# Retention in pairs of units, k tokens left out, and a shorter float64 conversion in a kernel of retention and two feed-forward layers

## The chip, the core and the metric

The kernel runs on one core of a Trainium2 chip, in one launch. The metric is the device time of that launch in microseconds, the median of several runs. The core's engines are named as in the profile: PE (matmul) with PEld (its weight loads), DVE (VectorE), ACT (ScalarE), POOL (GpSimd) and SP (SyncE, here only a queue of DMAs). 16 DMA engines move data.

## What is computed

Batch 4, 8 heads, 768 tokens, head size 64; then two feed-forward layers on 3072 tokens of width 512, inner width 2048, in float32:

```python
gamma = 1.0 - 2.0 ** (-5.0 - np.arange(H))
for t in range(S):
    state = gamma[None, :, None, None] * state + np.einsum('bhd,bhe->bhde', k[:, :, t], v[:, :, t])
    y[:, :, t] = scale * np.einsum('bhd,bhde->bhe', q[:, :, t], state)
x = y.transpose(0, 2, 1, 3).reshape(B * S, H * D)
h = x @ w_in;   x = (h * (1.0 / (1.0 + np.exp(-1.702 * h)))) @ w_out       # first layer
h = x @ w_in2;  x = (np.maximum(h, 0.0) ** 2) @ w_out2                     # second layer
```

q, k and v come as float32, the four weight matrices as float64.

## The kernel before

**Retention.** It runs over 24 units of 128 tokens (`NU`; six, `CPB`, in each of four batch rows). A unit's data are 2048 float32 words in each of 128 partitions, 1 MB: words 0 to 1023 are q and k transposed (`qk`), 1024 to 1535 the k tokens (`kn`), 1536 to 2047 v. `load_unit` (L462) brings them in two DMAs of 512 KB on SP's queue into one of five buffers (`UNITS`), and the load of unit u + 4 stands behind the outputs of unit u - 1. `scores(u)` (L489) makes the products of k and q (`sc`, 16 matmul instructions on 64 rows by 128 columns), the masked copy `pt` on DVE, and `vs`, v times a decay, on POOL for units below 6 and every third one, else on ACT as eight small multiplications. `outputs(u)` (L547) makes on PE: `yp` from `vs` and `pt` (array shape 128 by 64), the growth of the state `dp` from `kn` and `vs` (128 by 64; not for the sixth unit of a batch row, whose state no one reads), which ACT copies to `st`, and the part of `yp` across units from `st` and q (64 by 64; not for the first unit of a batch row). `scaled` multiplies `yp` on DVE by a table into the layer's input: `x0` for block 0 (split by `split_0` into `hl`), `xs` or `xout` for the others. The loop at L610 does scores(u), then outputs(u - 1). In PSUM `sc` has one buffer and `yp` two.

**Weights.** A float64 word is turned into float32 from its two 32-bit halves. `scale_words` (L131) scales the upper half as a float and the lower half as an integer, both on ACT; `join` (L138) shifts and masks the upper half and then puts the sign back, two DVE operations; `round_up` (L150) adds the lower half, a third. `cv_high` (ACT) and `cv_low` (DVE) split the result into two fp32r parts, hi and lo, in `w`. The first layer has 32 such slices (`order`), loaded by POOL's queue (`cv_load`, 512 KB each, five buffers `raw`). `cv_unit` (L193) does the steps of one slice over three units from unit 7 on (`CV0`), six slices in all during the retention; the other 26 are done by `cv_step` (L216) beside block 0.

**First layer.** Blocks 0 and 1 of 512 tokens go through `up` (L647: 12 matmuls, gelu and its copy on ACT, the rest `gl` on DVE) and `down` (L676: 12 matmuls, two steps behind), 16 steps each. In block 0 each step calls `cv_step` twice, every fourth step once. Slices of `up(f)` are number 2f - 1 of `order`, those of `down(f)` number 2f + 2. After that, blocks of 1024 tokens run in a product scheme with seven products for eight quadrants (`up2`, `down2`); their operands are made by `make_first` and `make_second` beside the earlier blocks, in pieces that `background` draws by credit in us. `make_second` (L331) converts the 32 slices of the second layer's weights with the same `scale_words`, `join` and `round_up`. Its 384 and 128 columns have opposite signs.

The order on each engine is the order in which the code is written (`tc.manual_schedule`); the waits between engines follow from tiles and their buffers.

Of the kernel before, what the change touches and what calls it, by code (L numbers as in the profile page):

```python
# [19 lines left out]
P = 128  # L20
# [13 lines left out]
UNITS = 5  # L34
# [11 lines left out]
CV0 = 7  # L46
RAWU = 2
# [17 lines left out]
def tile_retention_then_two_ffns(  # L65
# [65 lines left out]
    def scale_words(hm, raw, n=512):  # L131

        nc.scalar.mul(hm[:, 0:n], raw[:, 0:n, 1].bitcast(F32), 2.0 ** -112)
        if n < 512:
            nc.scalar.mul(hm[:, n:512], raw[:, n:512, 1].bitcast(F32), -2.0 ** -112)
        nc.scalar.mul(raw[:, :, 0], raw[:, :, 0], 2.0 ** -29)  # L136

    def join(out, hb):  # L138

        v.tensor_scalar(  # L140
            out=out, in0=hb, scalar1=3, scalar2=0x7FFFFFFF,
            op0=ALU.logical_shift_left, op1=ALU.bitwise_and,
        )
        yield
        v.scalar_tensor_tensor(
            out=out, in0=hb, scalar=0x80000000, in1=out, op0=ALU.bitwise_and, op1=ALU.bitwise_or
        )
        yield

    def round_up(w, raw):  # L150

        half = w.bitcast(U16).rearrange("p (c t) -> p c t", t=2)[:, :, 0]
        v.scalar_tensor_tensor(out=half, in0=half, scalar=65527.0, in1=raw[:, :, 0], op0=ALU.min, op1=ALU.add)
# [24 lines left out]
    def convert():  # L178
# [7 lines left out]
        for _ in join(hm.bitcast(U32), raw[:, :, 1]):  # L186
            yield
# [5 lines left out]
    def cv_unit(u):  # L193

        cv["step"] += 1
        part = (u - CV0) % 3
        if part == 2:
            cv_low()
        elif part == 1 and half:
            next(half.pop(), None)  # L200
        elif part == 0 and u >= CV0 and cv["b"] < cv["a"]:
            half.append(convert())
            next(half[0])
            next(half[0])

    def cv_ahead(u):

        if u == 21:
            cv["ahead"] = RAWS
        if u >= RAWU and (u - RAWU) % 3 == 0 or u > 21:  # L210
            cv_load()
        n = cv["a"]
        if n < min(cv["load"], cv["b"] + 2) and cv["step"] >= loaded[n] + 4:
            cv_a()

    def cv_step(f=None):  # L216
# [3 lines left out]
        if cv["b"] < cv["a"]:  # L220
            for _ in convert():
                pass
# [108 lines left out]
    def make_second():  # L331

        with (
# [27 lines left out]
            for n in range(len(jobs)):  # L361
# [5 lines left out]
                hb = hm.bitcast(U32)  # L367
                w = pool.tile([P, 8, P], F32, tag="w", name=f"w32_{n}")
                wf = w.rearrange("p q c -> p (q c)")[:, 0:512]
                wu = wf.bitcast(U32)  # L370
# [841 lines left out]
```

## Time and profile before

| what | us |
|---|---|
| median of 3 runs | 1033.64 (1032.73 to 1034.77) |
| profiled execution, own time | 1033.87 |
| its span, first to last instruction | 1031.8 |
| PE busy | 1021.9 (99%), 5575 matmul records |
| PEld busy | 843.6 (82%) |
| DVE busy | 770.2 (75%) |
| ACT busy | 579.0 (56%) |
| POOL busy | 111.5 (11%) |

PE's busy time is a union of matmuls that overlap in the pipeline, so 99% says that it seldom stood with nothing under way, not that it ran at its peak. The profile names the granted clock of TensorE: 1.0 of full speed (2.4 GHz, the upper of its two levels) in all 40 slices of the span. The span has three parts: the retention to 82.8 us, blocks 0 and 1 of the first layer, and the blocks of the product scheme. In the retention the rows to look at are PE's groups and the DMA share; behind it, what the weight loads (PEld) waited for, since all other idle time of the other engines costs nothing.

### The profile page before, as it was taken

What the parts mean: (1) busy time and instruction counts of PE and PEld (TensorE: products, weight loads), DVE (VectorE), ACT (ScalarE), POOL (GpSimd) and SP (SyncE); (2) the same over time, 40 slices, a digit from 0 to 9 for tenths busy, and PEclk for the clock granted to TensorE, in tenths of its full rate; (3) what the DMA queues carried; (4) which work ended last, traced back from release to release, by engine and by line L of the source; (5) the groups of instructions that cost most, each with busy time, mean ns of one, the idle gap of its engine ahead of it and who ended that gap; (6) DMA issues with size and microseconds to landing.
All of it is one profiled execution on the core that took longest, in us unless ns stands there. A gap on an engine that the chain in (4) does not pass through costs nothing.

```text
span 1031.8 us, 15634 instructions
## 1 busy us (share of the span) xinstructions
PE 1021.9 (99%) x5575; PEld 843.6 (82%) x5575; DVE 770.2 (75%) x1033; ACT 579.0 (56%) x960; POOL 111.5 (11%) x167
## 2 busy tenths in 40 slices
PE   8999999999999999999999999999999999999998
PEld 6888888888888888888888888888888888888886
DVE  5888998798888888666888776886455986455953
ACT  4767775344667565566655798564233464334443
POOL 3121110111322000211001211000000001000000
PEclk9999999999999999999999999999999999999999
DMA  9994797866879887999886999867666867766664
GB/s 356 407 398 173 263 314 296 320 229 242 308 233 373 300 293 233 363 368 364 269 289 228 389 381 307 261 221 237 214 194 191 266 223 235 216 192 194 213 195 163
DMA packets 118669, 281.38 MB, mean 273 GB/s; under 512 B 12608, under 2 KB 12736, under 8 KB 118336
## 3 DMA queue, kind: packets, MB, share of 16 engines
q1 hardware_dynamic: 93200, 186.95, 54.3%
q0 software_dynamic: 24672, 92.28, 24.9%
q10 hardware_dynamic: 720, 1.15, 0.3%
q8 instruction: 44, 0.72, 0.3%
q14 instruction: 33, 0.27, 0.1%
HBM read 206.93 MB, written 73.40 MB: 272 GB/s over the span
## 4 chain that ended last, share of the span: by engine, by line
PE 80%; DVE 2%; ACT 1%; DMA 1%; issue 0%; DVEq 0%
PE D L893 36%; PE X L893 17%; PE Z L893 8%; PE Y L893 4%; PE y L685 2%; PE y L684 2%; PE y L683 2%; PE h L652 2%; PE h L654 1%; PE h L653 1%; PE h L856 1%; PE h L855 1%; PE h L854 1%; DMA r<-kw 1%; DVE wq L350 0%
## 5 line engine op out<-in xcount | busy, mean ns | idle before, releaser
L893 PE MATMUL D<-gx,r 128*128 128x512 f32 x1680 | 383.5, 389 | 0.1
L893 PEld LDWEIGHTS D<-gx,r 128*128 128x128 f32 x1680 | 314.9, 188 | 67.0 <-DVE gx L998 1.2
L998 DVE TENSOR_TENSOR gx<-g,gx 128x1024 fp32r<-128x1024 f32 x140 | 170.9, 1223 | 43.9 <-ACT gx L997 43.4
L997 ACT CAST gx<-g 128x1024 fp32r<-128x1024 f32 x140 | 146.0, 1054 | 95.1 <-PE D L893 91.8
L893 PE MATMUL X<-xh,r 128*128 128x512 f32 x576 | 177.9, 390 | 0.3 <-ACT g L911 0.2
L911 ACT COPY g<-X 128x512 f32<-128x512 f32 x108 | 63.4, 587 | 153.6 <-PE X L893 153.6
L916 DVE TENSOR_TENSOR g<-Z,g 128x512 f32<-128x512 f32 x72 | 49.7, 690 | 128.8 <-ACT g L911 98.7
L893 PEld LDWEIGHTS X<-xh,r 128*128 128x128 f32 x576 | 107.7, 188 | 24.2 <-ACT g L911 1.8
L893 PE MATMUL X<-xl,r 128*128 128x512 f32 x288 | 112.0, 389 | 0.0
L893 PE MATMUL Z<-xh,r 128*128 128x512 f32 x288 | 88.7, 389 | 0.0
L893 PEld LDWEIGHTS X<-xl,r 128*128 128x128 f32 x288 | 54.0, 188 | 11.4
L893 PEld LDWEIGHTS Z<-xh,r 128*128 128x128 f32 x288 | 54.1, 188 | 11.2
L893 PE MATMUL Z<-xl,r 128*128 128x512 f32 x144 | 56.0, 389 | 0.0
L652 PE MATMUL h<-hl,w 128*128 128x512 f32 x128 | 50.1, 392 | 0.3 <-DVE w L173 0.2
L653 PE MATMUL h<-hl,w 128*128 128x512 f32 x128 | 49.9, 390 | 0.0
L654 PE MATMUL h<-hl,w 128*128 128x512 f32 x128 | 49.8, 389 | 0.0
L685 PE MATMUL y<-gl,w 128*128 128x512 f32 x128 | 49.8, 389 | 0.0
L683 PE MATMUL y<-gh,w 128*128 128x512 f32 x128 | 49.8, 389 | 0.0
L684 PE MATMUL y<-gh,w 128*128 128x512 f32 x128 | 49.8, 389 | 0.0
L351 POOL DMA_DIRECT2D kw<-wq x32 | 30.3, 947 | 151.4 <-DVE w L382 75.0
L893 PE MATMUL Y<-xh,r 128*128 128x512 f32 x144 | 44.3, 389 | 0.0
L136 ACT ACTIVATE raw<-raw 128x512 uint32<-128x512 uint32 x64 | 43.0, 672 | 0.0
(112 smaller groups left out, 1548.2 us busy)
## 6 DMA issues: line engine op xcount, KB each, us to landing
r<-kw SPq DMA_DIRECT2D x532, 256.0 KB, 3.3
kw<-wq POOLq DMA_DIRECT2D x32, 896.0 KB, 7.1
unit<-qkv SPq DMA_DIRECT2D x48, 512.0 KB, 9.1
raw<-w POOLq DMA_DIRECT2D x32, 512.0 KB, 6.2
kw<-wh POOLq DMA_DIRECT2D x16, 1024.0 KB, 4.7
kw<-w SPq DMA_DIRECT2D x16, 512.0 KB, 4.7
raw<-win POOLq DMA_DIRECT2D x16, 512.0 KB, 6.8
raw<-wout POOLq DMA_DIRECT2D x16, 512.0 KB, 7.9
```

Source lines behind the costliest of these rows:

```text
L136: nc.scalar.mul(raw[:, :, 0], raw[:, :, 0], 2.0 ** -29)
L652: nc.tensor.matmul(hp, lo[:, k], xh, start=(k == 0), stop=False)
L653: nc.tensor.matmul(hp, hi[:, k], xh, start=False, stop=False)
L654: nc.tensor.matmul(hp, hi[:, k], xl, start=False, stop=(k == KD - 1))
L683: nc.tensor.matmul(a, lo[:, e], gh, start=s0, stop=False)
L684: nc.tensor.matmul(a, hi[:, e], gh, start=False, stop=False)
L685: nc.tensor.matmul(a, hi[:, e], gl, start=False, stop=s1)
L893: nc.tensor.matmul(a, w, b, start=start, stop=stop, skip_group_check=True)
L911: nc.scalar.copy(out=t, in_=a)
L916: v.tensor_tensor(out=t, in0=a, in1=t, op=ALU.add)
L997: nc.scalar.copy(out=hi, in_=src)
L998: v.tensor_tensor(out=lo, in0=src, in1=hi, op=ALU.subtract)
```

## The change

- The retention goes over groups: units 0 and 1 alone, then pairs. Both scores of a pair stand together, then the outputs of the pair before, in the order: state of its first unit, values of both, state of the second, across for both. `sc` has two buffers, one for even and one for odd units; `yp` has one, of twice the use: both units of a pair share the tile. `pt` and `vs` have four buffers. `vs` of even units goes to POOL, of odd ones to ACT (units below 6 all to POOL).
- Eight units may be held instead of five; five of each eight lie in buffers of the weight pool `wa`, free at that time. A unit's load is split at the tile border, and for the sixth unit of a batch row the k tokens are not loaded.
- The conversion uses a parametric relu (one ACT pass that scales positive and negative upper halves differently, so that the shift brings the sign in its place), one shift on DVE, and one operation that scales and adds the lower half's upper 16 bits. ACT passes over the lower half are gone.
- Four slices are converted in the retention, one per group from group 8 on; in block 0 each step calls `cv_step` twice. The credit that `make_second` reports for a slice is 1.65 instead of 1.85 us.

```diff
-UNITS = 5
+UNITS = 8
+WIDE = 5
-CV0 = 7
-RAWU = 2
+CV0 = 8
+RAWU = 4
+CONV = 4
...
     def scale_words(hm, raw, n=512):
-        nc.scalar.mul(hm[:, 0:n], raw[:, 0:n, 1].bitcast(F32), 2.0 ** -112)
-        if n < 512:
-            nc.scalar.mul(hm[:, n:512], raw[:, n:512, 1].bitcast(F32), -2.0 ** -112)
-        nc.scalar.mul(raw[:, :, 0], raw[:, :, 0], 2.0 ** -29)
+        for a, z, scale in ((0, n, 2.0 ** -112), (n, 512, -2.0 ** -112)):
+            if a < z:
+                nc.scalar.activation(
+                    out=hm[:, a:z], in_=raw[:, a:z, 1].bitcast(F32), func=ACTF.Prelu, scale=scale, alpha=-2.0 ** 32
+                )
     def join(out, hb):
-        v.tensor_scalar(
-            out=out, in0=hb, scalar1=3, scalar2=0x7FFFFFFF,
-            op0=ALU.logical_shift_left, op1=ALU.bitwise_and,
-        )
-        yield
-        v.scalar_tensor_tensor(
-            out=out, in0=hb, scalar=0x80000000, in1=out, op0=ALU.bitwise_and, op1=ALU.bitwise_or
-        )
-        yield
+        v.tensor_scalar(out=out, in0=hb, scalar1=3, scalar2=None, op0=ALU.logical_shift_left)
...
-        v.scalar_tensor_tensor(out=half, in0=half, scalar=65527.0, in1=raw[:, :, 0], op0=ALU.min, op1=ALU.add)
+        half = halves(w.bitcast(U16))[:, :, 0]
+        low = raw.bitcast(U16).rearrange("p c (t u) -> p c t u", u=2)[:, :, 0, 1]
+        v.scalar_tensor_tensor(out=half, in0=low, scalar=2.0 ** -13, in1=half, op0=ALU.mult, op1=ALU.add)
...
-    def cv_unit(u):
+    def cv_group(k):
         cv["step"] += 1
...
+        cv_low()
+        if k >= CV0 and cv["b"] < min(cv["a"], CONV):
+            convert()
+    def cv_ahead(k):
+        if k >= RAWU:
             cv_load()
         n = cv["a"]
-        if n < min(cv["load"], cv["b"] + 2) and cv["step"] >= loaded[n] + 4:
+        if n < min(cv["load"], cv["b"] + 2) and cv["step"] >= loaded[n] + 2:
             cv_a()
...
-                    units[u] = att.tile([P, 2048], F32, tag="unit", name=f"unit{u}", bufs=UNITS)
+                    units[u] = [
+                        wa_p.tile([P, 1024], F32, tag=f"w{i}", name=f"unit{u}_{i}")
+                        if u % UNITS >= UNITS - WIDE
+                        else att.tile([P, 1024], F32, tag=f"unit{i}", name=f"unit{u}_{i}", bufs=UNITS - WIDE)
+                        for i in range(2)
+                    ]
...
+                    if a == 1024 and u % CPB == CPB - 1:
+                        a = 1536
...
-                if u == 1:
-                    sc = aps.tile([P, 2, NP, P], F32, tag="yp", name="sc1")
-                else:
-                    sc = aps.tile([P, 2, NP, P], F32, tag="sc", name=f"sc{u}", bufs=1)
+                sc = aps.tile([P, 2, NP, P], F32, tag=f"sc{u % 2}", name=f"sc{u}", bufs=1)
...
-                if u < CPB or u % 3 == 0:
+                if u < CPB or u % 2 == 0:
...
-                yp = aps.tile([P, 2, NP, P], F32, tag="yp", name=f"yp{u}")
+                yp = aps.tile([P, 2, NP, P], F32, tag="yp", name=f"yp{pair[0]}", bufs=1)
...
+                grow(pair[0])
+                for g, u in enumerate(pair):
+                    within(g, u)
+                for u in pair[1:]:
+                    grow(u)
+                for g, u in enumerate(pair):
+                    across(g, u)
...
-            for u in range(NU + 1):
-                cv_high()
-                masked = scores(u) if u < NU else None
+            groups = [(0,), (1,)] + [(u, u + 1) for u in range(2, NU, 2)]
+            for k, group in enumerate(groups + [()]):
+                masks = [scores(u) for u in group]
...
                 low = split_0()
-                scaled = outputs(u - 1) if u > 0 else None
+                before = groups[k - 1] if k > 0 else ()
+                scaled = outputs(before) if before else None
...
+                cv_high()
+                for masked in masks:
                     masked()
                 if low is not None:
                     low()
-                cv_unit(u)
+                cv_group(k)
                 if scaled is not None:
                     scaled()
-                cv_ahead(u)
-                if u > 0:
-                    load_unit(u + UNITS - 1)
+                cv_ahead(k)
+                for u in before:
+                    load_unit(u + UNITS)
...
                 cv_step(low)
-                if f % 4 < 3:
-                    cv_step()
+                cv_step()
...
-                steps = join(wu, hb)
-                next(steps)
-                yield 0.45
-                next(steps)
-                yield 0.7
+                join(wf.bitcast(U32), hm.bitcast(U32))
+                yield 0.6
                 round_up(wf, raw)
                 later(lambda n=n: load(n + 3))
-                yield 0.7
+                yield 1.05
```

How the instructions stand, at three places. First PE at the end of the retention, before (`sc` scores, `yp` values from `pt` and `vs` or across from `st`, `dp` state; the numbers are buffers; in brackets the engines and DMA queues waited for):

```order
L499 MATMUL sc_1308<-unit_1155 128x128 [waits DMAHW0_49,DVE_49]
L499 MATMUL sc_1308<-unit_1155 128x128 x7
L556 MATMUL yp_1327<-pt_1263,vs_1264 64x128 [waits Activation_49] x8
L567 MATMUL dp_1138<-vs_1264,unit_1107 64x64 [waits DMAHW7_49,Activation_49]
L567 MATMUL dp_1138<-vs_1264,unit_1107 64x64 x7
L578 MATMUL yp_1327<-unit_1107,st_1290 64x128 x8
L556 MATMUL yp_1360<-pt_1317,vs_1318 64x128 [waits DVE_49,Activation_49]
L556 MATMUL yp_1360<-pt_1317,vs_1318 64x128 [waits Activation_49] x7
L578 MATMUL yp_1360<-unit_1155,st_1344 64x128 [waits Activation_49]
L578 MATMUL yp_1360<-unit_1155,st_1344 64x128 x7
```

And now, from the state of unit 20, just behind the last scores, to the values of the last pair:

```order
L559 MATMUL dp_1149<-vs_1127,unit_1_917 64x64 [waits DMAHW3_49,Activation_49,Pool_49]
L559 MATMUL dp_1149<-vs_1127,unit_1_917 64x64 x7
L573 MATMUL yp_1238<-pt_1126,vs_1127 64x128 [waits DVE_49,PE_49]
L573 MATMUL yp_1238<-pt_1126,vs_1127 64x128 x7
L573 MATMUL yp_1238<-pt_1138,vs_1139 64x128 x8
L559 MATMUL dp_1149<-vs_1139,unit_1_921 64x64 [waits DMAHW5_49,Activation_49]
L559 MATMUL dp_1149<-vs_1139,unit_1_921 64x64 x7
L588 MATMUL yp_1238<-unit_0_916,st_1184 64x128 x8
L588 MATMUL yp_1238<-unit_0_920,st_1247 64x128 x8
L559 MATMUL dp_1149<-vs_1217,unit_1_1023 64x64 [waits DMAHW7_49,Activation_49,Pool_49]
L559 MATMUL dp_1149<-vs_1217,unit_1_1023 64x64 x7
L573 MATMUL yp_1298<-pt_1216,vs_1217 64x128 [waits DVE_49,PE_49]
```

Behind the last scores stood the outputs of two units; now the outputs of two pairs do, and the values of the last pair wait for DVE, which reads the one `yp` buffer.

POOL's queue at the same place, before (`vs` of units 15, 18 and 21 by their loads, `raw` the weight slices):

```order
L518 TENSOR_TENSOR vs_924<-unit_765,tab_sb 128x512 [waits PE_49,DMAHW1_49,Activation_49,Pool_49]
L127 DMA raw_1067<-w 128x1024 [waits DMASW0_49,DVE_49]
L518 TENSOR_TENSOR vs_1083<-unit_910,tab_sb 128x512 [waits PE_49,DMAHW7_49,Activation_49,Pool_49]
L127 DMA raw_1207<-w 128x1024 [waits DMASW1_49,DVE_49]
L518 TENSOR_TENSOR vs_1220<-unit_1069,tab_sb 128x512 [waits PE_49,DMAHW5_49,Activation_49,Pool_49]
L127 DMA raw_1306<-w 128x1024 [waits DMASW2_49,DVE_49]
L127 DMA raw_1357<-w 128x1024 [waits DMASW3_49,DVE_49]
L127 DMA raw_1379<-w 128x1024 [waits DMASW4_49,DVE_49]
```

And now (`vs` of units 18, 20 and 22):

```order
L508 TENSOR_TENSOR vs_1040<-unit_1_817,tab_sb 128x512 [waits DMAHW7_49,PE_49,Pool_49]
L129 DMA raw_1114<-w 128x1024 [waits DMASW0_49,DVE_49,Activation_49]
L508 TENSOR_TENSOR vs_1127<-unit_1_917,tab_sb 128x512 [waits DMAHW3_49,PE_49,Pool_49]
L129 DMA raw_1204<-w 128x1024 [waits DMASW1_49,DVE_49,Activation_49]
L508 TENSOR_TENSOR vs_1217<-unit_1_1023,tab_sb 128x512 [waits DMAHW7_49,PE_49,Pool_49]
L129 DMA raw_1381<-w 128x1024 [waits DMASW2_49,DVE_49,Activation_49]
L129 DMA raw_1390<-w 128x1024 [waits DMASW3_49,DVE_49,Activation_49]
```

The slices behind the last `vs` stand behind unit 22 instead of unit 21; seven slices stand ahead of it, as many as before.

DVE in a step of block 0, before (`hm` the joined slice, `gl` the low part of the gelu, `w` the low part of a slice):

```order
L140 TENSOR_SCALAR hm_1457<-raw_1357 128x512 [waits DMASW0_49,DVE_49,Activation_49]
L145 SCALAR_TENSOR_TENSOR hm_1457<-raw_1357,hm_1457 128x512 [waits DVE_49]
L153 SCALAR_TENSOR_TENSOR hm_1457<-hm_1457,raw_1357 128x512 [waits DVE_49,Activation_49]
L664 TENSOR_TENSOR gl_1_1453<-gs_1_1451,gh_1_1452 128x512 [waits Activation_49]
L173 TENSOR_TENSOR w_1429<-hm_1428,w_1429 128x4x128 [waits Activation_49]
L140 TENSOR_SCALAR hm_1469<-raw_1379 128x512 [waits DMASW1_49,DVE_49,Activation_49]
```

And now:

```order
L143 TENSOR_SCALAR hm_1448<-raw_1390 128x512 [waits DMASW0_49,DVE_49]
L152 SCALAR_TENSOR_TENSOR hm_1448<-raw_1390,hm_1448 128x512 [waits DVE_49]
L696 TENSOR_TENSOR gl_2_1444<-gs_2_1442,gh_2_1443 128x512 [waits PE_49,Activation_49]
L172 TENSOR_TENSOR w_1422<-hm_1421,w_1422 128x4x128 [waits DMAHW4_49,DMAHW2_49,Activation_49]
L143 TENSOR_SCALAR hm_1458<-raw_1418 128x512 [waits DMASW1_49,DVE_49]
```

A slice takes three operations on DVE where it took four, in the same places of the row.

## Rows read from the trace of the kernel before

**Rows 1.** Busy time by stretch: PE, PEld, DVE, ACT, POOL; clock, DMA share, GB/s

```profile
60.00:74.00 14.00, 13.16 (x258) 11.63 (x256) 11.56 (x15) 8.61 (x28) 2.27 (x3) 1.00 1.03 408
74.00:83.00 9.00, 9.00 (x189) 7.70 (x186) 7.64 (x12) 7.98 (x24) 2.48 (x5) 1.00 0.79 274
83.00:170.00 87.00, 86.66 (x380) 70.99 (x381) 79.21 (x131) 63.91 (x112) 13.27 (x25) 1.00 0.72 249
```

**Rows 2.** Timeline of one unit on PE: start, us, engine, line, tiles, count

```profile
59.12 1.16 PE L499 MATMUL sc<-unit 64*128 64x128 f32 x16
...
60.22 1.09 PE L556 MATMUL yp<-pt,vs 128*64 128x128 f32 x16
...
61.14 0.63 PE L567 MATMUL dp<-vs,unit 128*64 128x64 f32 x16
...
61.70 0.67 PE L578 MATMUL yp<-unit,st 64*64 64x128 f32 x16
...
62.30 1.16 PE L499 MATMUL sc<-unit 64*128 64x128 f32 x16
```

**Rows 3.** DMA from 6 to 74 us: totals, SP's queue q1, POOL's q0

```profile
DMA packets 7606, 27.57 MB, mean 405 GB/s; under 512 B 840, under 2 KB 840, under 8 KB 7595
...
q1 hardware_dynamic: 6587, 23.74, 87.9%
q0 software_dynamic: 1008, 3.67, 13.6%
```

**Rows 4.** The last unit's two loads: issue and landing, from the tile's own view

```profile
L468 SPq DMA_DIRECT2D unit<-qkv x2: 328/380/432, 67.7 to 68.1; - x2
...
DMA to landing us min/median/max: 9.2/9.6/10.1
```

**Rows 5.** Timeline of POOL: issue of three weight slices

```profile
74.31 1.64 POOL L127 DMA_DIRECT2D raw<-w  x3
```

**Rows 6.** Timeline of the retention's end on ACT, PE and DVE

```profile
78.29 2.03 ACT L523 ACTIVATE vs<-unit,tab_sb 128x64 f32<-128x64 f32 x8
...
81.21 1.09 PE L556 MATMUL yp<-pt,vs 128*64 128x128 f32 x16
...
82.24 0.67 PE L578 MATMUL yp<-unit,st 64*64 64x128 f32 x16
...
82.83 0.50 PE L652 MATMUL h<-hl,w 128*128 128x512 f32 x1
...
82.97 0.69 DVE L595 TENSOR_TENSOR xout<-yp,ytab 128x512 f32<-128x512 f32 x1 [0.33 <-PE yp L578]
```

**Rows 7.** DVE groups to 82 us: busy us, mean ns | idle before

```profile
L508 DVE TENSOR_TENSOR pt<-sc,tab_sb 128x1024 f32<-128x1024 f32 x24 | 29.4, 1223 | 14.9 <-PE sc L499 14.8
...
L595 DVE TENSOR_TENSOR xout<-yp,ytab 128x512 f32<-128x512 f32 x7 | 4.8, 689 | 0.6 <-PE yp L578 0.5
```

**Rows 8.** DVE groups from 82 to 160 us

```profile
L153 DVE SCALAR_TENSOR_TENSOR hm<-hm,raw 128x512 uint16<-128x512 uint16 x25 | 19.1, 765 | 2.6
L145 DVE SCALAR_TENSOR_TENSOR hm<-raw,hm 128x512 uint32<-128x512 uint32 x25 | 17.3, 693 | 0.9
L173 DVE TENSOR_TENSOR w<-hm,w 128x512 fp32r<-128x512 f32 x25 | 17.1, 684 | 0.0
L140 DVE TENSOR_SCALAR hm<-raw 128x512 uint32<-128x512 uint32 x25 | 10.7, 427 | 2.1
L664 DVE TENSOR_TENSOR gl<-gs,gh 128x512 fp32r<-128x512 f32 x14 | 9.5, 682 | 1.7 <-ACT gh L660 1.7
```

**Rows 9.** ACT groups from 82 to 160 us: the gelu

```profile
L659 ACT ACTIVATE gs<-h 128x512 f32<-128x512 f32 x15 | 8.8, 587 | 7.9 <-DVE gl L664 4.9 <-PE h L654 3.0
```

**Rows 10.** Waits of weight loads, 83 to 162 and 163 to 1031 us: total, times, longest

```profile
PEld h L652 <- DVE w L173: 1.2, 2, 0.6
...
PEld X L893 <- ACT g L911: 1.8, 4, 0.6
```

**Rows 11.** ACT groups of the first 6 us: the table load

```profile
L476 ACT ACT_TABLE_LOAD x1 | 1.3, 1283 | 1.2 <-PEq L1202 1.2
```

More of the change, by code (lines that the diff above doesn't have):

```diff
@@ L185, in convert @@
         w = wpool[key[0]].tile([P, 4, 2, P], F32R, tag=f"w{key[1]}", name=f"w{n}")
[L186 to L187 removed]
+        join(hm.bitcast(U32), raw[:, :, 1])
         round_up(hm, raw)
@@ L220, in cv_step @@
         if cv["b"] < cv["a"]:
-            for _ in convert():
-                pass
+            convert()
         if f is not None:
@@ L460, in tile_retention_then_two_ffns @@
             units = {}
+            state = {}
+            snaps = {}
+            first = []
+            pend = {}
             def load_unit(u, parts=(0, 1024, 2048)):
@@ L542, in split_0 @@
-                return low
+                blocks = list(first)
+                first.clear()
+                for xt, cols in blocks:
+                    for k in range(KD):
+                        nc.scalar.copy(out=hl[0][k][0][:, cols], in_=xt[:, k, :])
+                def low():
+                    for xt, cols in blocks:
+                        for k in range(KD):
+                            hi, lo = hl[0][k]
+                            nc.vector.tensor_tensor(
+                                out=lo[:, cols], in0=xt[:, k, :], in1=hi[:, cols], op=ALU.subtract
+                            )
@@ L570, in outputs, with within, across @@
                             )
-                    ns = att.tile([P, NP, D], F32, tag="st", name=f"st{u}")
+                    ns = att.tile([P, NP, D], F32, tag="st", name=f"st{u}", bufs=3)
                     nc.scalar.copy(out=ns, in_=dp)
                     state[b] = (dp, ns)
-                if c > 0:
+                    snaps[u + 1] = ns
+                def within(g, u):
+                    pt, vs = pend[u]
+                    for p in range(NP):
+                        for r in range(2):
+                            nc.tensor.matmul(
+                                yp[64 * r:64 * r + 64, p % 2, 2 * g + p // 2, :], vs[:, 2 * p + r, :],
+                                pt[:, r ^ p % 2, p, :],
+                                start=(g == 0 and p < 2), stop=(u % CPB == 0), skip_group_check=True,
+                            )
+                def across(g, u):
+                    st = snaps.pop(u, None)
+                    if st is None:
+                        return
+                    qk = views(u)[0]
                     for p in range(NP):
@@ L584, in outputs, with scaling @@
-                if 0 < j < XHELD and o == 0:
-                    xs[j] = block_tiles(f"x{j}")
-                def scaled():
+                grow(pair[0])
[5 more added lines that the diff above has]
+                    across(g, u)
+                def scaling(g, u):
+                    b, c = divmod(u, CPB)
+                    j, o = divmod(u, UPB)
+                    cols = slice(o * P, (o + 1) * P)
+                    if 0 < j < XHELD and o == 0:
+                        xs[j] = block_tiles(f"x{j}")
@@ L599, in scaled @@
-                        pend["x"] = (xt, cols)
+                        v.tensor_tensor(out=banked(xt), in0=y, in1=banked(ytab_sb[c]), op=ALU.mult)
+                        first.append((xt, cols))
+                def scaled():
+                    for g, u in enumerate(pair):
+                        scaling(g, u)
+                for u in pair:
+                    units.pop(u)
+                    pend.pop(u)
                 return scaled
```

103 lines of the change are left out of this document (38 added, 65 removed).

## Prediction

> **What bounds the kernel now.** I read the busy table cut by stage, then the tensor engine's timeline in the retention, the DMA totals, and last the waits of the weight loads. The profiled execution took 1033.87 us with a span of 1031.8, so 2.07 us lie around the span; it stands 0.23 us above the median of 1033.64, which I neglect. The reader is to see three things. First, from 83 us on the tensor engine (PE) hardly rests: 380 matmuls in 87 us, 0.23 us apart, at full granted clock [rows 1], and the weight loads waited only a few microseconds in all [rows 10]. That part can give back those waits and no more. Second, the retention before it, which ends at 82.83 us [rows 6], has two limits close together. PE needs 3.18 us per unit of 128 tokens, from one scores group to the next [rows 2]. The 16 DMA engines are full too: 27.57 MB in 68 us, 405 GB/s, of it 23.74 MB units and 3.67 MB seven weight slices [rows 3], at a share of 1.03 until 74 us and only 0.79 after it [rows 1]. Third, the end of the retention hangs on the last unit: its two loads are issued at 67.7 and 68.1 and land 9.2 and 10.1 us later, at 76.9 and 78.2 [rows 4]; its vs on ACT begins at 78.29 [rows 6].
>
> **Pairs on PE.** 16 matmuls of 128 columns take 0.92 us until the next group when that uses the same array shape (128 rows by 64 columns, 60.22 to 61.14), and 1.10 (59.12 to 60.22) or 1.03 (81.21 to 82.24) when the shape changes [rows 2, 6]. A change of shape therefore costs 0.11 to 0.18 us. A unit has three of them (scores, then state and values, then across), a pair in the new order also three, so three go per pair: 0.33 to 0.54 us, 3.6 to 5.9 us in eleven pairs. That is PE's side alone; it counts only where the data are there before PE is.
>
> **Loads.** The k tokens of units 5, 11, 17 and 23 are not read: 128 x 512 words of 4 bytes, 0.262 MB each. Three lie ahead of unit 23's first half: 0.79 MB at 405 GB/s is 1.9 us. The slices give nothing there: seven were loaded before 74 us, and in the new order seven still stand ahead of unit 22's vs on GpSimd. What differs is the next three, issued from 74.3 on [rows 5], 2.6 us before the last unit's first half landed, sharing the engines with it; now they stand behind the vs of unit 22. For that I take 0.9 us, between 0 and 1.9 (half of the 3.9 us from their issue to 78.2). Unit 23's first half then lands at 76.9 - 1.9 - 0.9 = 74.1 (73.1 to 75.0).
>
> That eight units may be under way instead of five moves nothing while the engines are full, and here a rule is weighed against the edit. The DMA share is 1.03 until 74 us [rows 1]. The Trainium skill, DMA: Bandwidth & Descriptors, section Issuing engines are not separate DMA queues, says that DMAs started by any engine end on the same 16 DMA engines and interleave. By that rule earlier issue is worth nothing and the sum below holds; without it PE's side would decide, which is the first rival. The trace agrees so far: the slices of GpSimd's queue and the units of SP's make up the 405 GB/s together.
>
> **The tail of a pair.** After the last scores more is left now. From the start of unit 23's scores at 74.2: scores 1.10, state of unit 20 0.45 (0.56 [rows 2] less the 0.11 of a change that is not there), values twice 0.92, state 0.56, across 0.49 and 0.60: 5.04 us. Then comes the last group, with no scores before it. There is one yp buffer where there were two, so its values wait until VectorE (DVE) has scaled the pair before, and the rest of the retention and all of block 0 are queued behind that wait on PE. The scaling starts 0.14 us after PE went on (82.83 to 82.97 [rows 6]), two scalings take 0.69 each [rows 7], with 0.1 for the semaphore 1.62 us, of which the state of unit 22 covers 0.45. Then values 0.92 and 1.03, across 0.49 and 0.60: 3.04. In all 5.04 + 1.62 + 3.04 = 9.7 us, and block 0 starts at 83.9 instead of 82.83 [rows 6]: **+1.1 us** (0 to +2.0 by the landing; -0.9 if in addition DVE and ACT save a microsecond on the way; below that the first rival). In earlier steps the yp wait is covered: masks twice 1.22 and scalings 1.4 [rows 7] and a conversion 1.9 (0.43, 0.77, 0.68 [rows 8]) fill 5.7 of a step's 6 us on DVE, and scores and state (2.5 us) stand ahead of the values that need yp.
>
> Costed at nothing: the vs of even units on GpSimd and of odd ones on ACT. On ACT its 2.03 us [rows 6] stand ahead of the state copies. For unit 23 (v 0.65 us behind the first half) they end at 74.8 + 2.0 + 0.4 = 77.2; PE asks for them at 74.2 + 1.1 + 0.45 + 1.84 = 77.6. A landing later by 0.4 us uses the cover up, and each further tenth is then paid.
>
> **Block 0.** Before, two slices per step cost DVE twice 0.43 + 0.69 + 0.77 + 0.68 and one gl of 0.68 [rows 8], 5.8 us, against 24 x 0.23 = 5.5 us of PE; it did seven in four steps, and PE's weight loads still waited 1.2 us in two places for a converted slice [rows 10]. Without the second join operation (0.69) two slices cost 4.4 us. I take 0.9 of the 1.2 us back (0 to 1.2): **-0.9 us**. The ACT pass over the low words goes as well; ACT has room there. The new rounding reads 16-bit words further apart; nothing here shows it. The old one, 0.77 us for as many elements, is nearest; 0.5 to 1.2 us would still fit.
>
> **The second layer's slices.** The same two operations go from each of 32 slices made beside the later blocks. PE's weight loads waited there 1.8 us for copies on ACT that stand in one queue with such work [rows 10]. I take 1.0 back (from -0.5, since the work starts one step earlier and is asked for at other places, to 1.8): **-1.0 us**.
>
> **Sum.** 1033.87 + 1.1 - 0.9 - 1.0 = 1033.1 us.
>
> **Rivals.** *PE decides.* If units land before PE asks for them, the eleven pairs give 3.6 to 5.9 us less the 1.2 us of yp wait: about -3.5, and with the other terms 1033.87 - 3.5 - 1.9 = 1028.5 us. For it: PE was busy 9.00 of 9.00 us from 74 to 83 [rows 1]. Against it: the share of 1.03 and the landing at 78.2, which cannot come forward by more than its bytes. It decides if unit 23's first half lands before 82.83 - 3.5 - 9.7, about 70. Chance 0.17.
>
> *The later gains fail.* The retention's +1.1 stays, and the waits of block 0 and the second layer return in other places: 1033.87 + 1.1 = 1035.0. Nothing bars it: PE waits where ACT and DVE happen to stand in a queue. Chance 0.13.
>
> *Block 0 starves.* Four slices are ready at its start, not six. The fourth step needs slice 5 after three up groups and a down group of 12 matmuls: 48 x 0.23 = 11.0 us. On DVE the last scalings end at 1.6, slice 4 at 2.8; the first gelu and its copy end at 4.2 (up group 2.8, ACT twice about 0.6 [rows 9] and hops); then gl 0.7, slice 5 1.2, the subtraction of slice 4 0.7, slice 6 1.2, gl 0.7 and the subtraction of slice 5 0.7 end at 9.4. The slack is 1.6 us. Past it a step that needs a late slice waits about one conversion, 1.2 us: two such give 2.4, with block 0's 0.9 not gained: 1033.87 + 1.1 + 2.4 - 1.0 = 1036.4, slower than before. For it: the chain crosses ACT, DVE and PE eight times, and 0.2 us more per hop uses the slack up. Against it: each later step gains 1 us. Chance 0.13.
>
> *The table is loaded again.* If the parametric relu were not in the set loaded for the gelu, every change between them would be a load of 1.28 us [rows 11]. Two per step of block 0 add 2.6 us to ACT's 4.0 (63.9 us busy in 87 [rows 1], 5.5 per step): 1.1 over, in 14 steps 15 us, so 1048 or more. The built order has one table load at its start, as before. The Trainium skill, ScalarE: Activation LUTs, section Table sets, names relu, copy and identity among the members of every set, does not name the parametric relu, and gives about 2.66 us for a change of set; by that price it would be an estimated 54 us. The trace shows one load, at 1.28 us, and no more. Chance 0.02, and 0.05 for what I have not thought of.
>
> **How the numbers follow.** The forecast has 0.50, at 1033.1. About 0.2% (2.07 us) is what a measurement here can tell from no change: faster is below 1031.6, slower above 1035.7. Faster: the first rival 0.17, the lower end of the forecast 0.06, the unknown 0.02: 0.25. Slower: 0.10 of the starving, 0.02 of the table, 0.02 of the unknown: 0.14. Within: 0.61. The range goes to the first rival's value below and to the starving's above, leaving about half of each out: 1028.5 to 1036.3. The forecast alone has 1031.0 to 1034.9.
>
> **What would show it.** Unit 23's first half landing near 74 and PE idle ahead of the last two scores groups; a yp wait of about 1.2 us inside the last output group; block 0 starting at 83 to 85; no weight load waiting for w in block 0; fewer weight loads waiting behind ACT later. It is wrong if block 0 starts before 81 (PE decided), if a step of block 0 waits for slice 5 or 7, or if ACT shows a second table load.

## The result and the profile after

The changed kernel takes **1044.34 us** (median of 4 runs, 1043.30 to 1045.52), the kernel before, measured beside it, 1033.24: a ratio of 1.0105 (95% interval 1.0088 to 1.0123). It is slower by 11 us, where 1033.1 was forecast. The profiled execution took 1045.52 us with a span of 1043.5; the span before was 1031.8.

From the first matmul of block 0 on, both kernels issue the same 4152 matmuls in the same order on PE. So the start of each in the one trace less its start in the other is a ledger of where the time went. How much later (us) the changed kernel starts the same matmul:

| place (us in the trace of before) | later by | what was added since |
|---|---|---|
| block 0's first matmul, 82.8 | 2.8 | the retention, +2.8 |
| start of block 1, 160.3 | 1.8 | block 0, -0.95 |
| 255.1, last matmul before the mixed stage (PE goes over from block 1 to the product scheme) | 1.8 | nothing |
| 259.0, second group of twelve matmuls after it | 9.3 | **+7.5** |
| 424.6 | 11.2 | gaps at 338 to 349, +2.1, less 0.2 before them |
| 583.7 | 12.7 | one gap at 591, +1.8, less 0.2 before it |
| last matmul, 1027.6 | 11.7 | gaps of before that are gone, -1.0 |

**The retention's end**, the answer to [rows 6]. Timeline of PE in the changed kernel: start, us, engine, line, tiles, shapes, count, idle before.

```profile
68.16 2.06 PE L489 MATMUL sc<-unit 64*128 64x128 f32 x32
...
73.57 2.48 PE L489 MATMUL sc<-unit 64*128 64x128 f32 x32
75.98 0.69 PE L559 MATMUL dp<-vs,unit 128*64 128x64 f32 x16
77.19 1.97 PE L573 MATMUL yp<-pt,vs 128*64 128x128 f32 x32 [0.52 <-DVE xout L617]
78.96 0.66 PE L559 MATMUL dp<-vs,unit 128*64 128x64 f32 x16
79.55 1.10 PE L588 MATMUL yp<-unit,st 64*64 64x128 f32 x32
80.58 0.69 PE L559 MATMUL dp<-vs,unit 128*64 128x64 f32 x16
82.67 1.97 PE L573 MATMUL yp<-pt,vs 128*64 128x128 f32 x32 [1.40 <-DVE xout L617]
84.57 1.10 PE L588 MATMUL yp<-unit,st 64*64 64x128 f32 x32
85.60 0.50 PE L684 MATMUL h<-hl,w 128*128 128x512 f32 x1
```

The values (yp) wait twice for a scaling (xout) on DVE. What stands ahead of those scalings shows on DVE's timeline of the same stretch:

```profile
74.07 0.69 DVE L172 TENSOR_TENSOR w<-hm,w 128x512 fp32r<-128x512 f32 x1 [2.24 <-ACT w L167]
74.68 0.42 DVE L143 TENSOR_SCALAR hm<-raw 128x512 uint32<-128x512 uint32 x1
75.13 0.74 DVE L152 SCALAR_TENSOR_TENSOR hm<-raw,hm 128x512 uint16<-128x512 uint16 x1
75.77 1.27 DVE L617 TENSOR_TENSOR xout<-yp,ytab 128x512 f32<-128x512 f32 x2
76.96 2.34 DVE L498 TENSOR_TENSOR pt<-sc,tab_sb 128x1024 f32<-128x1024 f32 x2
80.63 0.69 DVE L172 TENSOR_TENSOR w<-hm,w 128x512 fp32r<-128x512 f32 x1 [1.33 <-ACT w L167]
81.25 1.28 DVE L617 TENSOR_TENSOR xout<-yp,ytab 128x512 f32<-128x512 f32 x2
```

PE had finished the first of these two pairs by 73.6, but its scaling starts at 75.77, behind a slice's conversion (lines 172, 143, 152). For the last unit's landing PE hardly waits: the 32 scores of the last pair take 2.48 us where those of the pair before take 2.06, so the wait is 0.4 us at most.

The last unit's loads, the answer to [rows 4], from the tile's own view of 60.0 to 62.5 us; 60.4 + 14.0 = 74.4 and 61.9 + 13.5 = 75.4:

```profile
L464 SPq DMA_DIRECT2D unit<-qkv x2: 328/328/328, 60.4 to 61.9; - x2
...
DMA to landing us min/median/max: 13.5/13.7/14.0
```

**Block 0**, the answer to [rows 1] and [rows 8]: busy time by stretch (PE, PEld, DVE, ACT, POOL; clock, DMA share, GB/s), then DVE's new rounding from 85 to 160 us. PE is busy 84.00 of 84.00 us.

```profile
86.00:170.00 84.00, 84.00 (x372) 69.54 (x371) 68.55 (x117) 51.51 (x91) 15.75 (x28) 1.00 0.79 278
```

```profile
L152 DVE SCALAR_TENSOR_TENSOR hm<-raw,hm 128x512 uint16<-128x512 uint16 x28 | 21.2, 756 | 1.0
```

**The 7.5 us at 257.** ACT's timeline there; L137 is the Prelu, `raw<-raw` a slice of the second layer, L738 the cast of the mixed stage's operands:

```profile
249.53 0.76 ACT L137 ACTIVATE raw<-raw 128x384 f32<-128x384 f32 x2
...
258.69 0.75 ACT L137 ACTIVATE raw<-raw 128x384 f32<-128x384 f32 x2 [6.59 <-DMA raw<-win]
259.35 0.57 ACT L691 ACTIVATE gs<-h 128x512 f32<-128x512 f32 x1
259.95 0.62 ACT L692 CAST gh<-gs 128x512 fp32r<-128x512 f32 x1
260.48 1.99 ACT L738 CAST xh<-x 128x1024 fp32r<-128x1024 f32 x2
```

The gelu of step 15 and the casts stand behind a Prelu that waits 6.59 us for its slice. The chain that ended last, from 248 to 270 us, tells why the slice is late (start, us, what):

```profile
249.26 0.75 DMA kw<-wh
250.02 4.06 issue
...
254.67 3.94 DMA raw<-win
```

The slice is the third (`load(2)`). Its buffer lies where the first generator held its last sums, and those are still being stored: the store, issued at 249.26, lands 4.7 us later. Only then is the load issued (254.67), to land 3.94 us after that. The instructions on ACT in the built order, before and after (names cut to their numbers of slice and step):

```
before                                  after
gh_14  (gelu's copy, step 14)           raw_0  Prelu
wh_7                                    gs_14, gh_14
raw_0  three scalings                   raw_1  Prelu
gs_15, gh_15                            wq_0
xh, xh (casts of the mixed stage)       raw_2  Prelu   <- load not landed
                                        gs_15, gh_15
                                        xh, xh
```

Before, one slice of the second layer stands ahead of the casts; after, three. The end of its scalings and the casts on ACT's timeline of before:

```profile
249.69 0.67 ACT L136 ACTIVATE raw<-raw 128x512 uint32<-128x512 uint32 x1
...
253.17 2.00 ACT L707 CAST xh<-x 128x1024 fp32r<-128x1024 f32 x2
```

In the changed kernel PE waits 4.3 us, and then its clock is low as well. Busy time by stretch as above, and two matmuls of the slow stretch on PE's timeline:

```profile
257.00:262.00 5.00, 0.73 (x3) 0.43 (x2) 2.24 (x4) 3.28 (x6) 0.39 (x1) 0.87 1.00 364
262.00:268.00 6.00, 5.96 (x15) 4.19 (x15) 1.91 (x2) 0.46 (x1) 0.00 (x0) 0.54 0.43 163
```

```profile
261.57 0.79 PE L885 MATMUL h<-xh,w 128*128 128x512 f32 x1 [4.27 <-ACT xh L738]
...
264.70 0.63 PE L885 MATMUL h<-xh,w 128*128 128x512 f32 x1
265.13 0.63 PE L886 MATMUL h<-xh,w 128*128 128x512 f32 x1
```

From 262 to 268 us the granted clock is 0.54, so for nearly the whole stretch the lower of its two levels (1.2 and not 2.4 GHz), and a matmul starts every 0.43 us instead of 0.23. Of the 7.5 us, 4.4 are idle time and 3.1 the slow matmuls after it.

### The profile page after: what moved, and what is told of

Same layout as the page of the kernel before. It is cut to its first block, busy times and chain, and to the rows that moved or that the text cites. A ratio compares the mean times of both kernels' runs of the same rounds, so it can differ in the third digit from the quotient of the medians.

```text
span 1043.5 us, 15465 instructions
## 1 busy us (share of the span) xinstructions
PE 1024.0 (98%) x5575; PEld 845.9 (81%) x5575; DVE 727.7 (70%) x969; ACT 535.5 (51%) x872; POOL 115.4 (11%) x170
## 4 chain that ended last, share of the span: by engine, by line
PE 73%; DMA 1%; issue 1%; ACT 0%; DVE 0%; POOLq 0%; ACTq 0%
PE D L924 37%; PE X L924 18%; PE Z L924 9%; PE Y L924 5%; PE h L885 2%; PE h L887 1%; PE h L886 1%; DMA r<-kw 1%; DMA raw<-win 0%; DVE wq L339 0%; PE y L714 0%; ACT xh L738 0%; PE y L715 0%; PE y L716 0%; ACT wq L373 0%
## 5 line engine op out<-in xcount | busy, mean ns | idle before, releaser
L924 PEld LDWEIGHTS D<-gx,r 128*128 128x128 f32 x1680 | 314.9, 188 | 67.2 <-DVE gx L1029 1.4
L924 PEld LDWEIGHTS Z<-xh,r 128*128 128x128 f32 x288 | 53.9, 188 | 13.5 <-DVE w L371 1.7
L924 PEld LDWEIGHTS X<-xl,r 128*128 128x128 f32 x288 | 54.1, 188 | 11.3
L137 ACT ACTIVATE raw<-raw 128x384 f32<-128x384 f32 (+1 forms) x96 | 46.1, 515 | 12.2 <-DMA raw<-win 6.7
```

Source lines behind the costliest of these rows:

```text
L137: nc.scalar.activation(out=hm[:, a:z], in_=raw[:, a:z, 1].bitcast(F32), func=ACTF.Prelu, scale=scale, alpha=-2.0 ** 32)
L924: nc.tensor.matmul(a, w, b, start=start, stop=stop, skip_group_check=True)
```

## The experiments

Each ratio is against the kernel before measured beside it (medians 1033.2 to 1033.7). The ledger is at the end of this section.

**The generator one step later.** In the changed kernel:

```
-    credit = [0.0]
+    credit = [-4.7]
```

> The changed kernel, with the generator that makes the second layer's slices starting one step (4.7 us of credit) later, as it stood before the change; nothing else differs. Theory A (a Prelu stands ahead of the xh casts in ACT's queue and waits for a slice that has not landed): the Prelu of the third second-layer slice now comes behind the xh casts, so the 4.4 us of idle PE near 257 us and the 3.1 us of half pace after it go: 1044.3 - 7.5 = 1036.8 us (1035.5 to 1038.5). Rival B (the loss comes from the slice's late landing itself, or from the new operations being slower, wherever the Prelu stands): at least 1042, with an idle PE of over 2 us between 250 and 275. Rival C (the half pace of PE after 262 us has nothing to do with the idle time): the idle goes, a stretch of matmuls 0.43 us apart stays, 1039 to 1041.

Measured: 1039.62 us, ratio 1.0057 (1.0042 to 1.0072). The stall is gone, and the slow matmuls with it: at 259.0 the kernel is 1.8 us late, not 9.3. That speaks for theory A, and against B and C. (The time lies in the range that C had named, but C's sign, matmuls 0.43 us apart, is absent.) But 2.8 us less came back than expected, so the time is above the range of A: new gaps stand at 426 to 436 and 586 to 610. Waits of PE from 424 to 437:

```profile
PE X L924 <- DMA r<-kw: 1.0, 2, 0.6
PE Z L924 <- DMA r<-kw: 0.4, 2, 0.3
PE Y L924 <- DMA r<-kw: 0.2, 1, 0.2
```

**One Prelu later.** The generator keeps its early start; only the place of the third slice's Prelu moves:

```
+                if n == 2:
+                    scale(n)
                 hm, done = hms.pop(n)
...
-                scale(n + 1)
+                if n != 1:
+                    scale(n + 1)
```

> The changed kernel with one move: the Prelu of the third second-layer slice (two instructions on ACT) is queued when that slice is due and not one slice ahead; in ACT's order it then stands behind the xh casts. The generator's pace and start stay those of the changed kernel. Theory A: the stall near 257 us goes with this alone, 1036 to 1038.5 us. Rival D (the earlier start itself makes the loss, through DVE or the queue of GpSimd, not the place of one Prelu): 1041 or more, with PE idle for another reason between 250 and 275.

Measured: 1037.84 us, ratio 1.0040 (1.0025 to 1.0054). ACT's timeline now has the casts at 255.53, and PE is busy without a break; the ledger stands at 2.4 us before the casts and behind them:

```profile
255.01 0.62 ACT L695 CAST gh<-gs 128x512 fp32r<-128x512 f32 x1 [1.22 <-PE y L718]
255.53 2.00 ACT L741 CAST xh<-x 128x1024 fp32r<-128x1024 f32 x2
```

```profile
257.00:262.00 5.00, 5.00 (x23) 4.13 (x22) 2.67 (x3) 0.55 (x2) 1.51 (x2) 1.00 0.88 262
262.00:268.00 6.00, 6.00 (x28) 4.98 (x27) 2.72 (x4) 4.39 (x9) 1.08 (x2) 1.00 1.02 404
```

Two instructions on ACT, moved behind the gelu, its copy, the two casts and four more, give back 6.5 us. Rival D falls: the early start does no harm there by itself. That the load is late is no matter either, as long as nothing urgent stands behind the instruction that needs it.

**The conversion alone.** The kernel before with the new conversion (new `scale_words`, `join`, `round_up`); the charge for one conversion stays 1.85 us. Of its edit, the place where the generator reports that charge:

```
-                steps = join(wu, hb)
-                next(steps)
-                yield 0.45
-                next(steps)
-                yield 0.7
+                join(wu, hb)
+                yield 0.8
                 round_up(wf, raw)
                 later(lambda n=n: load(n + 3))
-                yield 0.7
+                yield 1.05
```

> The kernel before the change with only the conversion of the float64 slices changed (Prelu on ACT instead of two scalings, one join operation instead of two, the new rounding); retention, the pace of block 0's conversion and the credit of the generator (1.85 us for the conversion of a second-layer slice) stay as before. By the prediction's terms block 0 gives back 0.9 and the second layer's slices 1.0: 1033.2 - 1.9 = 1031.3 us. If the conversion is worth nothing where the pace is not changed: 1033.2. If only block 0 gains: 1032.3. If the new operations cost more than the old ones: 1034 or more.

Measured: 1031.88 us (10 runs), ratio 0.9986 (0.9977 to 0.9995): a gain of 1.8 us by the medians. The trace gives 0.7 in the retention (block 0 starts at 82.1), for which the forecast's sum has no term, 1.0 in block 0, and 1.4 after 300 us: 0.5 at 319.6 and 0.9 between 598 and 630, places where the weight loads of before wait for ACT [rows 10]. That makes 3.2, but this one execution was 1.2 us below the median. So both terms for the conversion show at their places, while the close agreement of the median's 1.8 with their sum of 1.9 is in part luck.

**The old charge.** The held generator, and the sum charged for a conversion 1.85 again:

```
-                yield 0.6
+                yield 0.8
                 round_up(wf, raw)
...
-    credit = [0.0]
+    credit = [-4.7]
```

> The changed kernel with the generator held back by one step, as in the run with the later start, and with 1.85 us charged again for the conversion of a second-layer slice instead of 1.65. From the first xh cast on, ACT's order is then that of the kernel with the conversion alone. Theory P (the cheaper charge lets slices come closer together, so that their stores and loads meet the fetches of weights in other places: 2.4 us of gaps between 426 and 436 and 2.2 us between 586 and 610): these go, and the time is 1033.7 + 2.8 (retention) - 0.9 (block 0) - 1.5 (what the conversion alone gave after block 0) = 1034.1 us (1033.3 to 1035.5). Rival Q (these gaps come from the retention in pairs or are chance): 1038 or more.

Measured: 1035.61 us (10 runs), ratio 1.0019 (1.0009 to 1.0028), 0.1 us above the range named, and 4.0 us below the run with the held generator alone. The gaps at 426 to 436 and 586 to 610 are gone; at 340 one is left that costs 1.5 us by the ledger. So the 0.2 us in the charge are worth 4 us. With the cheaper charge 31 slices are converted between 262 and 620 us instead of 30, and PE waits for weights (r) in stretches where the DMA share is above 1. The share from 424 to 437 us is 1.04 in both kernels; why the weights come late in one of them only stays open.

**The retention: scaling before conversion.**

```
+                if scaled is not None:
+                    scaled()
                 cv_group(k)
-                if scaled is not None:
-                    scaled()
```

> The changed kernel with one exchange on VectorE in each step of the retention: the scaling of the pair before stands ahead of the slice conversion and not behind it. Theory T2 (the one yp buffer is held by conversion work that stands ahead of the scaling: 0.69 us ahead of the pair before the last, 0.36 us ahead of the last): both waits shrink and the masks come earlier; block 0 starts at 84.2 to 84.7 instead of 85.6, and the time is 1042.9 to 1043.5. Rival L (the landing of the last unit sets the end): 85.3 or later, 1044.0 or more. The stall near 257 us stays in both.

Measured: 1043.81 us, ratio 1.0099 (1.0084 to 1.0114); block 0 starts at 84.38. PE's timeline: the first wait is gone, the last is 0.89 instead of 1.40 us.

```profile
76.01 0.69 PE L559 MATMUL dp<-vs,unit 128*64 128x64 f32 x16
76.53 1.92 PE L573 MATMUL yp<-pt,vs 128*64 128x128 f32 x32
...
81.44 1.97 PE L573 MATMUL yp<-pt,vs 128*64 128x128 f32 x32 [0.89 <-DVE xout L617]
...
84.38 0.50 PE L684 MATMUL h<-hl,w 128*128 128x512 f32 x1
```

Theory T2 holds for the retention (84.2 to 84.7 expected), and rival L falls. The median is 0.3 us above the time named and not told apart from the changed kernel's. Four traces have the changed kernel's retention (the changed kernel, generator later, one Prelu later, and the old charge). In each of them 12.03 us pass from the last pair's first scores to block 0, though unit 23's first half lands anywhere from 72.4 to 74.7. With one Prelu later it was down at 72.4, 2.0 us sooner than in the changed kernel, and block 0 started at 86.19:

```profile
L467 SPq DMA_DIRECT2D unit<-qkv x1: 327/327/327, 60.8 to 60.8; - x1
...
DMA to landing us min/median/max: 11.6/11.6/11.6
```

With the scaling first it is 11.04 us.

**The retention: the last pair apart.**

```
-            groups = [(0,), (1,)] + [(u, u + 1) for u in range(2, NU, 2)]
+            groups = [(0,), (1,)] + [(u, u + 1) for u in range(2, NU - 2, 2)] + [(NU - 2,), (NU - 1,)]
```

> The changed kernel with the last pair of units (22, 23) as two groups of one unit; all else as changed. The stall near 257 stays. Theory T (the retention's loss of 2.8 us is made at its end, where the last values wait 1.6 us for the one yp buffer behind two scalings): with one scaling to wait for instead of two, and three more changes of the array's shape (0.4 us), block 0 starts at 84.2 to 85.0 instead of 85.6, and the time is 1043.0 to 1043.8. Rival L (the loss is set by the landing of the last units, and PE only waits in another place): block 0 starts at 85.4 or later, 1044.3 us or more.

Measured: 1045.11 us, ratio 1.0112 (1.0096 to 1.0127); block 0 starts at 85.8. A miss: one scaling instead of two shortens the last wait, but the conversion still stands ahead of the scaling in the group before, and unit 23 has a step of its own at the end. The length of the last wait alone was the wrong culprit; its place behind other work was the better one. Rival L had named such numbers, but not their cause: unit 23's first half landed at 75.0, and its scores began only at 79.5.

**The retention: with the k tokens.**

```
-                    if a == 1024 and u % CPB == CPB - 1:
-                        a = 1536
```

> The changed kernel with the k tokens of units 5, 11, 17 and 23 loaded again. If the landing of the last unit sets the retention's end in pairs too: the first half of unit 23 lands at 76.0 to 76.5 instead of 74.4 and block 0 starts at 87.0 to 87.6 instead of 85.6; 1045.8 to 1046.5 us. If the pair's tail sets it: under 86.2, 1044.3 to 1045.

Measured: 1045.49 us (2 runs), ratio 1.0115 (1.0094 to 1.0135). Unit 23's first half lands 14.1 us after its issue at 62.8, at 77.0 instead of 74.4, and block 0 starts at 87.34 instead of 85.60. The time is 0.3 us below the range named. PE's timeline now has a wait for the landing:

```profile
77.13 1.16 PE L487 MATMUL sc<-unit 64*128 64x128 f32 x16 [1.88 <-DMA unit<-qkv]
```

So with all bytes loaded the landing of the last unit sets the end of the pairs, and the bytes left out were worth 1.7 us. Of the 2.6 us by which it lands sooner without them 0.9 are lost: by then the order on DVE sets the end.

**Units one by one, conversion new, k tokens left out.** In the kernel with the conversion alone:

```
                 for a, z in zip(parts, parts[1:]):
+                    if a == 1024 and u % CPB == CPB - 1:
+                        a = 1536
```

> The kernel before with the conversion changed alone, and now also without the k tokens of units 5, 11, 17 and 23; units one by one as before. If the landing of the last unit decides (three k token tiles of 0.262 MB ahead of it at 405 GB/s: 1.9 us), block 0 starts at 80.2 to 80.8 instead of 82.1 and the time is 1030.0 to 1030.6. If the work on PE and VectorE decides, 81.6 or later and 1031.5 to 1032.

Measured: **1030.83 us** (9 runs), ratio 0.9972 (0.9962 to 0.9982), faster than both kernels. Its trace has block 0 at 81.0, between the two cases: the last half lands at 75.4 (67.2 + 8.2) instead of 77.9, but PE then has work left until 81.0 and no gap in the last units, and PE's 3.18 us per unit decide the last step. PE's timeline there:

```profile
76.20 1.16 PE L494 MATMUL sc<-unit 64*128 64x128 f32 x16
...
79.38 1.09 PE L551 MATMUL yp<-pt,vs 128*64 128x128 f32 x16
80.41 0.67 PE L573 MATMUL yp<-unit,st 64*64 64x128 f32 x16
81.00 0.50 PE L647 MATMUL h<-hl,w 128*128 128x512 f32 x1
```

**The changed kernel repaired**, with the held generator, the old charge and the scaling first; and the kernel above once more beside it.

> The changed kernel with the three repairs together: the generator one step later, 1.85 us charged for a conversion, and the scaling ahead of the conversion in the retention. If the losses are independent, block 0 starts near 84.4 us and the time is 1035.6 - 1.2 = 1034.4 us (1033.5 to 1035.2), still not below the kernel before, since the pairs end 1.5 us later and only 0.9 + 1.5 come back. If they are not (an earlier start of block 0 moves the second layer's slices to worse places), 1035.6 or more.

Measured: 1034.64 us (10 runs), ratio 1.0007 (0.9998 to 1.0017). The three repairs give back 9.7 us, and what is left is no gain. (Block 0 started at 85.2, not at 84.4. Its last unit landed at 75.3, 0.9 us later than in the changed kernel, but PE was 0.8 us late already at the scores of unit 22, and from there to block 0 10.8 us passed, no more than with the scaling first alone.)

> Units one by one with the new conversion and without the unused k tokens, measured once more beside the repaired version: 1030.8 us (1030.0 to 1031.5) if the first measurement holds, and 3 to 4 us below the repaired version.

Measured: 1030.63 us, ratio 0.9968 (0.9956 to 0.9981), as the first time and 4.0 us below the repaired kernel.

The ledger of all runs: how much later (us) than in the kernel before the same matmul starts, at the places of the first table.

| kernel | 82.8 | 160.3 | 259.0 | 424.6 | 583.7 | 1027.6 |
|---|---|---|---|---|---|---|
| changed | 2.8 | 1.8 | 9.3 | 11.2 | 12.7 | 11.7 |
| generator later | 2.8 | 1.8 | 1.8 | 1.3 | 5.6 | 6.0 |
| one Prelu later | 3.4 | 2.4 | 2.4 | 3.4 | 5.4 | 4.9 |
| later, old charge | 2.8 | 1.8 | 1.8 | 2.9 | 2.6 | 1.5 |
| scaling first | 1.5 | 0.6 | 7.9 | 8.5 | 10.1 | 9.0 |
| last pair apart | 3.0 | 2.0 | 9.3 | 10.3 | 12.2 | 11.3 |
| pairs with k | 4.5 | 3.5 | 10.5 | 10.9 | 12.6 | 11.5 |
| repaired | 2.3 | 1.4 | 1.3 | 3.0 | 2.7 | 1.6 |
| conversion alone | -0.7 | -1.7 | -1.8 | -2.2 | -2.0 | -3.2 |
| units, no k | -1.8 | -2.8 | -2.8 | -1.6 | -1.0 | -2.1 |

These are single executions; the places after 300 us differ by about 1 us between executions.

## Why the prediction was wrong

**The second layer's slices, -1.0: the step that failed.** The prediction counted what the new operations save on DVE and ACT, and knew that the work starts one step earlier. It let that pass as "asked for at other places", with a bound of 0.5 us of loss. The gain that it counted came: in the changed kernel too the ledger falls by 0.5 us at 319.6 and by 0.9 between 598 and 630. What failed is the bound on the loss: 11.4 us were lost (7.5 and 3.9, below), so that behind block 0, where -1.0 was forecast, the ledger rose by 9.9, from 1.8 to 11.7. The prediction did not follow the moved instructions to what stands behind them. Every slice that moves ahead takes its Prelu along in ACT's queue, ahead of the gelu of step 15 and the casts on which PE waits next; and the third slice can't be there, since its load needs the space of a store that is still under way. This costs 7.5 us; one Prelu moved back gives them back. The built order showed the three Prelu instructions ahead of the casts before any run, and the trace of before the 5.5 us from the last store to the first load behind it. The cheaper charge was not costed at all. It gives the gaps at 426 to 436 and 586 to 610 when the start is held. In the changed kernel itself the gaps at 338 to 349 and at 591 add 3.9 us more; that the charge makes these too is likely but not shown, since the old charge was not tried with the early start.

**Pairs and loads, +1.1: too small, it was 2.8; the yp wait was right, what sets its length was not.** The first half of unit 23 landed at 74.4 (74.1 forecast). Its scores began at 74.9 (75.98 less 1.10), 0.7 later than forecast. From there to the last group 5.7 us passed (5.04 forecast), since the yp wait that was costed at nothing "in earlier steps" was 0.7 us: the sum of DVE's work fits in a step, but the conversion stands ahead of the scaling. This is the second term that failed. The last group took 5.0 (4.66), since line 172's subtraction stands ahead of its scalings too. 0.68, 0.66 and 0.36 make the 1.7 that was missing, and the exchange on DVE gives 1.2 of it back (1.0 of it behind the last pair's first scores). An earlier landing alone would not have, as the 12.03 us show. Beside units one by one with the same conversion and the same bytes (block 0 at 81.0), the retention in pairs ends 4.6 us later as changed and 4.2 us later repaired; the slices converted in it differ as well, so not all of that need be the pairs'.

**Loads.** That the units' bytes decide, and not PE, was right as long as all bytes are loaded: with the k tokens back the end is 1.7 us later (1.9 forecast). In the changed kernel the loads still hold ACT up by 2.8 us at 68.5 (`vs` of unit 21); in the last pair the order on DVE decides. The rival by which PE decides fell; block 0 of the changed kernel started at 85.6, not before 81. That eight units under way move nothing held as well: with all bytes loaded, unit 23's first half lands at 77.0 in the kernel in pairs, at 76.9 before [rows 4], though it is issued five microseconds earlier. The Trainium skill, DMA: Bandwidth & Descriptors, section Issuing engines are not separate DMA queues, says that DMAs started by any engine run on the same 16 DMA engines and interleave. The two landings agree with what the prediction drew from it.

**Block 0, -0.9: right**, 0.95. No weight load waits for a slice there. The new rounding takes 0.756 us, 0.77 was taken.

**Block 0 starves; the table is loaded again.** Neither came. PE has no gap in block 0, and ACT's groups of the whole span have one table load:

```profile
L472 ACT ACT_TABLE_LOAD x1 | 1.3, 1283 | 1.2 <-PEq L1233 1.2
```

The 2.66 us for a change of set, quoted in the prediction from the Trainium skill, ScalarE: Activation LUTs, stand in its section What ACT_TABLE_LOAD costs; the section Table sets rounds them to 2.7, and no run here shows such a change.

**The rivals as a whole.** Of the rivals on the slow side two priced a loss, in block 0 (1036.4) and by table loads (1048 or more); the third, on the later gains, let them come to nothing (1035.0) and not turn into a loss. A forecast that names "PE waits where ACT and DVE happen to stand in a queue" has to look at which instruction stands ahead of the next stage's operands. Without that stall the time would have been 1036.8 (by the trace) to 1037.8 (by the run with one Prelu moved), still beyond the range, by the later gaps and the tail of the pairs.

## What to carry to other kernels

Where work in the background is made cheaper or started earlier, list what now stands in each engine's queue ahead of the next stage's first operands, and for each such instruction when its own data can land at the earliest; a wait there holds up all that stands behind it (here ACT for 6.59 us and PE for 4.3). Before two steps are merged, look not only at the sum of an engine's work in a step but at what stands ahead of the one instruction that frees the shared buffer. And try the parts apart: here the conversion and the bytes left out gave 2.6 us together, and the pairs and the new pace took them and eleven more.

## What was not expected of the hardware

A wait can cost more than its length. After the 4.3 us at 257 PE ran twelve matmuls at half pace, 3.1 us on top. The three other kernels that kept the early Prelu (scaling first, last pair apart, pairs with k) show the same: waits of 4.2 to 4.7 us, a granted clock of 0.51 to 0.71 from 262 to 268 us, and 7.0 to 7.4 us lost in all.

Shorter waits do not always have this effect. At 12 to 14 us the retention in pairs waits 2.2 us for a load (the longest wait of the retention before was 1.1 us), and in the changed kernel granted clocks of 0.73 and 0.50 follow. Timeline and busy time by stretch:

```profile
14.38 1.63 PE L489 MATMUL sc<-unit 64*128 64x128 f32 x16 [2.21 <-DMA unit<-qkv]
```

```profile
14.00:16.00 2.00, 1.61 (x18) 1.42 (x19) 0.00 (x0) 0.00 (x0) 0.48 (x2) 0.73 1.04 422
16.00:18.00 2.00, 2.00 (x29) 2.00 (x30) 1.95 (x5) 0.89 (x4) 0.64 (x1) 0.50 1.03 413
```

All eight traces of retentions in pairs have this wait, of 2.1 to 2.3 us; in six the clock falls, in two (generator later, scaling first) it stays at 1.00. It cost nothing at the end: with the generator later, at the full clock, the last pair's first scores start at 73.58, and in the changed kernel at 73.57. A gap of 1.48 us stands at 61 us in all four traces of the changed kernel's retention. With one Prelu later the clock from 62 to 64 us was 0.55 behind it, in the three others 1.00. The wait in the changed kernel, and that with one Prelu later:

```profile
60.64 0.87 PE L588 MATMUL yp<-unit,st 64*64 64x128 f32 x18 [1.48 <-issue]
```

```profile
61.00 0.86 PE L591 MATMUL yp<-unit,st 64*64 64x128 f32 x18 [1.48 <-issue]
```

PE's gap of 1.3 us at 591 in the changed kernel was followed by the full clock too (1.00 from 592 to 600 us). So the length of the gap alone does not tell it.
